# One quarter of the last values load in six transfers, with unread products moved

## The chip, the cores and the metric

The kernel runs on one core of a Trainium2 chip. The metric is device time in microseconds (us), the median of several executions. The profile is of one execution.

## The reference

The input is one decode step: x of 8 rows by 512. It is normalized to xn, and the output is x plus two branches of xn:

```python
q = (xn @ wq).reshape(8, 1, 32, 128).transpose(0, 2, 1, 3)
scores = einsum("bhqd,bhkd->bhqk", q, repeat(k_cache, 4)) * 128 ** -0.5
o = einsum("bhqk,bhkd->bhqd", softmax(scores), repeat(v_cache, 4))
A = o.transpose(0, 2, 1, 3).reshape(8, 1, 4096) @ wo
h = xn @ w1 + b1
B = (h * tanh(softplus(h))) @ w2
return x + A + B
```

The caches have 8 rows, 8 heads, 8192 positions and 128 values each, all float32: 268 MB of keys and 268 MB of values. Each byte is read once and used for the four query heads of its group.

## The kernel before

**Loads.** All large loads are issued by SyncE (SP) from one list. `plan` puts a load into `queue`; `pump` issues the loads at the head of the list for as long as their place is free; `release` gives a place free after the last use and calls `pump`. There are three places in SBUF: "a" (tile `kva`, 16 rows of 1024 floats a partition), "b" (`kvb`, 20 rows) and "w" (`kvw`, 4 rows). One load of keys or values is 8 MB, 128 partitions of 64 KB. Every `dma_start` of a load stands on line 121. The framework puts in all waits, and gives each transfer one of eight completion semaphores in turn (by number 102, 103, 105, 107, 108, 109, 110, 100).

**Work.** The batch of 8 and the 8 KV heads are cut into 16 packs of two batch rows (b = 0, 1) by two heads. For pack p the loop scores the keys of (p, b) (`scores`, L353), does the softmax (`maximum`, `exponents`, `fold`, `weights`) and multiplies the values of (p - 1, b) (`values`, L460, then `gather` L471 and L473). In `values` a round is four products into four column strips; the trace has two records for each float32 product, so a whole batch is 64 records.

**The tail** (L695 on) is the change's place. The values of the last pack's first batch come in place "b", those of its second batch in "a", in two parts by columns: three quarters, and the last quarter (16 KB in each of 128 partitions). Then come w2 in four parts (`W2_PARTS`, 8, 8, 8 and 4 KB a partition) and between them the last wo in two halves (8 KB each):

```python
    plan_v(PACKS - 1, 0, "b")
    plan_v(PACKS - 1, 1, "a", ((0, 3 / 4), (3 / 4, 1)))
    W2_PARTS = ((0, 2), (2, 4), (4, 6), (6, 7))
    for k, (lo, hi) in enumerate(W2_PARTS):
        plan("w2", "b", w2, ((lo / W2R, hi / W2R),))
        if 0 < k < 3:
            plan_wo(PAIRS - 1, (((k - 1) / 2, k / 2),))
```

So SP issues, in order: the values' three quarters, the last quarter, w2 part 0, w2 part 1, wo half 0, w2 part 2, wo half 1, w2 part 3, and the output (L719). TensorE's order in the tail is that of the code: `values(0)`, `sums`, `merge` (L488), `add_up` (L548), `values(1)` in two calls, `down` part 0 (L628), two unread products (`keep_busy`, L639), `merge`, `turn` (L514, copies on L526 and L528), `down` part 1, half of `last_outputs` (L562), `down` part 2, the other half, `down` part 3. All of it but the unread products adds into one PSUM tile H or leads to it; L718 copies H out.

`keep_busy(n)` multiplies `ones` by `acc` into C[0], which nothing reads any more. Each engine's order is held to that of the code by the loop at the end of the kernel.

Of the kernel before, what the change touches and what calls it, by code (L numbers as in the profile page):

```python
# [13 lines left out]
P = 128  # L14
# [26 lines left out]
PACKS = PAIRS * NP  # L41
R = P // G
HE = P // 2
# [29 lines left out]
def kernel(  # L73
# [12 lines left out]
    nc = tc.nc  # L86
# [9 lines left out]
    queue = []  # L96
    taken, landed = {}, {}

    def rows_of(blocks):

        return blocks.rearrange("j p f -> (j p f)").rearrange("(p f) -> p f", p=P)
# [9 lines left out]
        del taken[next(at for at, w in taken.items() if w == what)]  # L111
        pump()

    def plan(what, at, blocks, parts=((0, 1),), lo=0):

        rows = rows_of(blocks)
        n = rows.shape[1]
        t = place[at][:, lo : lo + n]

        def load(cols):  # L120
            nc.sync.dma_start(t[:, cols], rows[:, cols])
            return t

        for first, end in parts:
            cols = slice(round(first * n), round(end * n))
            queue.append((what, at, lambda cols=cols: load(cols)))


    sc = const.tile([P, 512], F32, name="sc")
# [7 lines left out]
    def blocks_of(src, p, b):  # L137
        i, k = divmod(p, NP)
        lo = ((k * PB + b) * HKV + 2 * i) * NB
        return src[lo : lo + KN]  # L140
# [3 lines left out]
    def plan_k(p, b):  # L144
        if (p, b) == (0, 1):
            plan(("k", p, b), "a", blocks_of(kT, p, b))
        else:
            up[0] = KX * BW - up[0]
            plan(("k", p, b), "b", blocks_of(kT, p, b), lo=up[0])

    def plan_v(p, b, at, parts=((0, 1),)):
        plan(("v", p, b), at, blocks_of(v, p, b), parts)

    def plan_wq(i):
        plan(("wq", i), "w", wq[i * CC : (i + 1) * CC])
# [11 lines left out]
    for p in range(PACKS):  # L167
        for b in range(PB):
            plan_k(p, b)
            if (p, b) in between:  # L170
                what, i = between[p, b]
                (plan_wq if what == "wq" else plan_wo)(i)
            if p > 0:
                plan_v(p - 1, b, "a")
    plan_v(PACKS - 1, 0, "b")
    plan_v(PACKS - 1, 1, "a", ((0, 3 / 4), (3 / 4, 1)))
    W2_PARTS = ((0, 2), (2, 4), (4, 6), (6, 7))
    for k, (lo, hi) in enumerate(W2_PARTS):
        plan("w2", "b", w2, ((lo / W2R, hi / W2R),))
# [274 lines left out]
    def values(b, vt, lo=0, hi=ROUNDS):  # L454


        for k in range(lo, hi):
            for c in range(G):
                j = G * k + c
                nc.tensor.matmul(  # L460
                    O[b][Q * c : Q * (c + 1), :],
                    pt[:, b, j % 2, j // 2].rearrange("p t e h -> p (t e h)"),
                    vt[:, W4 * DH * j : W4 * DH * (j + 1)],
                    start=(k == 0),
                    stop=(k == ROUNDS - 1),
                )
# [17 lines left out]
    def merge(p, b):  # L484

        i, k = divmod(p, NP)
        at = 168 + b * 2 * REP
        nc.tensor.matmul(M[:, at : at + 2 * REP], OS.pop((p, b)), hsel, start=True, stop=True)  # L488
        if b == PB - 1:
            if k == 0:  # L490
                oT[i] = work.tile([P, 2, REP, B], F32, name="oT")
            nc.vector.tensor_mul(  # L492
                oT[i][:, :, :, k * PB : (k + 1) * PB].rearrange("p e h b -> p (e h) b"),
                M[:, 168 : 168 + PB * 2 * REP].rearrange("p (b r) -> p r b", b=PB),
                RT.pop(p).rearrange("p b e h -> p (e h) b"),
            )
# [48 lines left out]
    def add_up():  # L545

        for g in range(G):
            nc.tensor.matmul(  # L548
                H[Q * g : Q * g + B, :P],
                rsel[:, :B],  # L550
                acc[:, g * P : (g + 1) * P],
                start=True,
                stop=False,
            )

    def last_outputs(lo, hi, w):

        for r in range(lo, hi):
            for h in range(2):
                for g in range(G):  # L560
                    at = r * BW + h * D + g * P
                    nc.tensor.matmul(  # L562
                        H[Q * g : Q * g + B, :P],
                        oW[PAIRS - 1][:, r, h, :],
                        w[:, at : at + P],
                        start=False,
                        stop=False,
                    )
# [54 lines left out]
    def down(lo, hi, w):  # L623

        for j in range(2 * lo, 2 * hi):
            for g in range(G):
                at = j * D + g * P
                nc.tensor.matmul(  # L628
                    H[Q * g : Q * g + B, :P],
                    aT[:, j, :B],  # L630
                    w[:, at : at + P],
                    start=False,
                    stop=(j == 2 * W2R - 1),
                )

    def keep_busy(n):

        for k in range(n):
            nc.tensor.matmul(C[0][:Q, :], ones[:, :Q], acc, start=True, stop=True)  # L639
# [19 lines left out]
    for p in range(PACKS):  # L659
        for b in range(PB):  # L660
            k = landed.pop(("k", p, b))
# [17 lines left out]
            if (p, b) in between:  # L679
                what, i = between[p, b]  # L680
# [14 lines left out]
    p = PACKS - 1  # L695
# [5 lines left out]
    sums(p, lsel.pop(p))  # L701
    merge(p, 0)
    add_up()
    values(1, landed["v", p, 1], 0, ROUNDS * 3 // 4)
    values(1, landed["v", p, 1], ROUNDS * 3 // 4)
    gather(p, 1)
    w2_sb, wo_sb = landed["w2"], landed["wo", PAIRS - 1]
    down(*W2_PARTS[0], w2_sb)
    keep_busy(2)
    merge(p, 1)  # L710
    turn(PAIRS - 1, tid)
    down(*W2_PARTS[1], w2_sb)
    last_outputs(0, OR // 2, wo_sb)
    down(*W2_PARTS[2], w2_sb)
    last_outputs(OR // 2, OR, wo_sb)
    down(*W2_PARTS[3], w2_sb)
    res = acc[:, :P]
# [59 lines left out]
```

## Time and profile before

| what | value |
|---|---|
| median of 3 runs | 1311.33 us (1311.27 to 1312.54) |
| the profiled execution | 1311.37 us |
| its span | 1309.6 us |
| TensorE matmul busy (PE) | 879.2 us, 67% |
| VectorE busy (DVE) | 385.2 us, 29% |
| ScalarE busy (ACT) | 111.6 us, 9% |
| loads' queue q1 | 561.06 MB, 99.3% of 16 engines |
| mean granted TensorE clock | 0.823 |

The span runs from the program's first instruction to its last; 1.8 us of the execution's time lie around it. Start times below are counted from the span's start. PE is a matmul, PEld its weight load. A line like "L460 PE" names the kernel's line and the engine. "DMA kvb<-in_w" is the transfer of w2 into place "b", "SPq" the issuing by SyncE.

### The profile page before, as it was taken

To read this page: it belongs to the slowest core of one execution; us is meant where nothing else is said; L and a number is where in the kernel's file an instruction comes from. 1 tells how busy PE (TensorE), PEld (TensorE's weight loads), DVE (VectorE), ACT (ScalarE), POOL (GpSimd) and SP (SyncE) were. 2 spreads that over 40 slices of the span, in tenths; PEclk is the share of its full clock that TensorE was granted. 3 is DMA by queue.
4 is the path that set the end of the run, shared out by engine and by line. 5 is a ranking of instruction groups with operands and counts; after the bars stand their busy time and mean duration, and the time that the engine had idled before them with its cause. 6 is when DMAs were issued, how large, how long until landed. Compare 5 with 4: busy or idle time off the path is not lost.

```text
span 1309.6 us, 10699 instructions
## 1 busy us (share of the span) xinstructions
PE 879.2 (67%) x4768; PEld 282.3 (22%) x4768; DVE 385.2 (29%) x590; ACT 111.6 (9%) x294; POOL 4.8 (0%) x10
## 2 busy tenths in 40 slices
PE   4886667866567766677666686665775666766567
PEld 1221112212112221122211222121221221222113
DVE  7150504205050230522305033052320505114051
ACT  1020101001010100101101010010100101001010
POOL 1000000000000000000000000000000000000000
PEclk9887788887789877797777887778887779878778
DMA  9999999999999999999999999999999999999997
GB/s 406 440 427 437 437 427 428 440 433 431 432 435 429 433 437 425 443 421 445 419 442 421 418 448 425 441 421 443 423 437 432 429 433 421 443 427 435 437 425 333
DMA packets 11590, 561.76 MB, mean 429 GB/s; under 512 B 1292, under 2 KB 1424, under 8 KB 1560
## 3 DMA queue, kind: packets, MB, share of 16 engines
q1 hardware_dynamic: 11520, 561.06, 99.3%
q8 instruction: 37, 0.61, 0.2%
q14 instruction: 9, 0.07, 0.0%
q10 hardware_dynamic: 24, 0.02, 0.0%
HBM read 561.01 MB, written 0.07 MB: 428 GB/s over the span
## 4 chain that ended last, share of the span: by engine, by line
DMA 61%; PE 35%; DVE 3%; issue 0%; ACT 0%; SPq 0%; DVEq 0%; ACTq 0%
DMA kvb<-in_kT 52%; PE c L353 30%; PE o L460 3%; DMA kva<-in_v 3%; DMA kva<-in_kT 3%; DMA kvb<-in_w 2%; DMA kvb<-in_v 2%; DVE raw L412 1%; DVE pt L430 1%; PE h L312 0%; PE o L581 0%; PE s L365 0%; DVE raw L421 0%; DVE nm L379 0%; DVE os L473 0%
## 5 line engine op out<-in xcount | busy, mean ns | idle before, releaser
L353 PE MATMUL c<-kvb,qT 128*64 128x512 f32 x1984 | 500.7, 669 | 334.4 <-DMA kvb<-in_kT 302.3
L353 PEld LDWEIGHTS c<-kvb,qT 128*64 128x64 f32 x1984 | 161.7, 154 | 673.3 <-issue 424.4
L460 PE MATMUL o<-kva,pt 128*32 128x512 f32 x1984 | 251.4, 665 | 26.2 <-DMA kva<-in_v 26.2
L379 DVE TENSOR_REDUCE nm<-s 128x1 f32<-128x1024 f32 x16 | 19.6, 1225 | 454.7 <-PE s L365 454.7
L412 DVE STREAM_TRANSPOSE raw<-e 128x2048 f32<-128x2048 f32 x32 | 116.2, 3630 | 14.3 <-ACT e L404 12.7
L460 PEld LDWEIGHTS o<-kva,pt 128*32 128x32 f32 x1984 | 67.1, 121 | 200.3 <-issue 161.1
L360 ACT COPY sc<-c 128x512 f32<-128x512 f32 x32 | 18.7, 585 | 1003.4 <-PE c L353 1003.4
L404 ACT ACTIVATE e<-s,nms 128x512 f32<-128x512 f32 x128 | 86.2, 685 | 126.3 <-DVE nms L393 66.8
L492 DVE TENSOR_TENSOR oT<-m,r 128x16 f32<-128x16 f32 x16 | 2.8, 174 | 234.1 <-PE m L488 234.1
L471 DVE TENSOR_SCALAR os<-o,isel 128x128 f32<-128x128 f32 x32 | 11.2, 351 | 160.1 <-PE o L460 160.1
L430 DVE TENSOR_TENSOR pt<-raw 64x256 f32<-64x256 f32 x128 | 53.6, 419 | 2.0
L365 PE MATMUL s<-sc,csel 64*128 64x512 f32 x128 | 38.0, 672 | 8.4 <-ACT sc L360 8.4
L421 DVE TENSOR_TENSOR raw<-raw 128x1024 f32<-128x1024 f32 x32 | 39.2, 1226 | 1.1
L340 DVE TENSOR_TENSOR qT<-qc,bsel 128x1024 f32<-128x1024 f32 x32 | 37.7, 1219 | 0.0
L473 DVE SCALAR_TENSOR_TENSOR os<-o,isel,os 128x128 f32<-128x128 f32 x96 | 33.7, 351 | 3.4
L404 ACT ACTIVATION_READ_ACCUMULATOR e<-s,nms 128x1 f32 x128 | 26.0, 203 | 0.0
L380 PE MATMUL m<-ident,nm 128*1 128x128 f32 x16 | 4.3, 270 | 21.2 <-DVE nm L379 21.2
L312 PE MATMUL h<-kvw,xnT 128*64 128x512 f32 x64 | 17.6, 699 | 0.0
L488 PEld LDWEIGHTS m<-hsel,os 128*128 128x128 f32 x64 | 9.5, 188 | 28.5 <-issue 24.4
L323 DVE TENSOR_SCALAR e<-h 128x512 f32<-128x512 f32 x16 | 9.9, 684 | 17.2 <-PE h L312 17.2
L488 PE MATMUL m<-hsel,os 128*128 128x8 f32 x64 | 12.4, 266 | 3.1 <-DVE os L473 1.6
L353 PE MATMUL c<-kva,qT 128*64 128x512 f32 x64 | 14.0, 593 | 0.6 <-DMA kva<-in_kT 0.6
(100 smaller groups left out, 164.6 us busy)
## 6 DMA issues: line engine op xcount, KB each, us to landing
kvw<-in_wq SPq DMA_DIRECT2D x4, 2048.0 KB, 30.4
kvw<-in_wo SPq DMA_DIRECT2D x3, 2048.0 KB, 29.6
kva<-in_v SPq DMA_DIRECT2D x1, 6144.0 KB, 26.1
kva<-in_w SPq DMA_DIRECT2D x1, 3584.0 KB, 15.7
kvb<-in_w SPq DMA_DIRECT2D x3, 1024.0 KB, 21.0
kva<-in_v SPq DMA_DIRECT2D x1, 2048.0 KB
kvw<-in_wo SPq DMA_DIRECT2D x2, 1024.0 KB, 24.8
kvb<-in_w SPq DMA_DIRECT2D x1, 512.0 KB
```

The source lines that it names most:

```text
L340: nc.vector.tensor_mul(qT[:, b], qc[:, k * PB + b] .rearrange("p r (o h) -> p r o h", o=1) .to_broadcast([P, KR, KN, REP]), bsel.rearrange ...
L353: nc.tensor.matmul(C[b][HE * c : HE * (c + 1), :], t[:, r], k[:, r * BW + c * 512 : r * BW + (c + 1) * 512], start=(r == order[0]), stop=( ...
L360: nc.scalar.copy(sc, C[b])
L365: nc.tensor.matmul(S[:, c * 512 : (c + 1) * 512], csel[HE * c : HE * (c + 1), b].rearrange("p u b h -> p (u b h)"), sc[HE * c : HE * (c + ...
L379: nc.vector.tensor_reduce(nm, S, axis=AX.X, op=ALU.max, negate=True)
L404: nc.scalar.activation(ex[:, :, s, :], S[:, c * 512 : (c + 1) * 512].rearrange("p (t f) -> p t f", t=HT), AF.Exp, bias=NMS[p][:, s : s + 1 ...
L412: nc.vector.transpose(raw.rearrange("p (m t r) -> p t m r", m=TW, t=HT), ex.rearrange("p t s (q m) -> p t m (s q)", m=TW),)
L421: nc.vector.tensor_add(raw[:, :, :n], raw[:, :, :n], raw[:, :, n:])
L430: nc.vector.tensor_add(pt[rows, b, c].rearrange("p m t e h -> p (m t) e h")[:, :, e], raw[rows, :, at : at + REP], raw[rows, :, V8 + at : ...
L460: nc.tensor.matmul(O[b][Q * c : Q * (c + 1), :], pt[:, b, j % 2, j // 2].rearrange("p t e h -> p (t e h)"), vt[:, W4 * DH * j : W4 * DH * ...
L473: nc.vector.scalar_tensor_tensor(os, O[b][:, DH * i : DH * (i + 1)], isel[:, i : i + 1], os, op0=ALU.mult, op1=ALU.add,)
L488: nc.tensor.matmul(M[:, at : at + 2 * REP], OS.pop((p, b)), hsel, start=True, stop=True)
```

## The change

The last quarter of the last values is no longer one transfer over 128 partitions but six: partitions 0 to 63, the even ones of 64 to 127 (32 rows), and the odd ones in four transfers of eight rows (65, 73, ..., 121; then from 67, 69 and 71, each in steps of eight). They carry the same bytes to the same places. Of the unread products, the two between `down` part 0 and `merge` go; four stand after `add_up`, one ahead of `down` part 2 and one ahead of the second half of `last_outputs`.

```diff
-    def plan(what, at, blocks, parts=((0, 1),), lo=0):
+    WHOLE = (slice(0, P),)
+    SPLIT = (slice(0, HE), slice(HE, P, 2)) + tuple(slice(HE + k, P, 8) for k in range(1, 8, 2))
+
+    def plan(what, at, blocks, parts=((0, 1),), lo=0, split=()):
...
-        def load(cols):
-            nc.sync.dma_start(t[:, cols], rows[:, cols])
+        def load(cols, of):
+            for ps in of:
+                nc.sync.dma_start(t[ps, cols], rows[ps, cols])
             return t
 
-        for first, end in parts:
+        for k, (first, end) in enumerate(parts):
             cols = slice(round(first * n), round(end * n))
-            queue.append((what, at, lambda cols=cols: load(cols)))
+            of = SPLIT if k in split else WHOLE
+            queue.append((what, at, lambda cols=cols, of=of: load(cols, of)))
...
-    plan_v(PACKS - 1, 1, "a", ((0, 3 / 4), (3 / 4, 1)))
+    plan_v(PACKS - 1, 1, "a", ((0, 3 / 4), (3 / 4, 1)), split=(1,))
...
     add_up()
+    keep_busy(4)
     values(1, landed["v", p, 1], 0, ROUNDS * 3 // 4)
     values(1, landed["v", p, 1], ROUNDS * 3 // 4)
     gather(p, 1)
     w2_sb, wo_sb = landed["w2"], landed["wo", PAIRS - 1]
     down(*W2_PARTS[0], w2_sb)
-    keep_busy(2)
     merge(p, 1)
     turn(PAIRS - 1, tid)
     down(*W2_PARTS[1], w2_sb)
     last_outputs(0, OR // 2, wo_sb)
+    keep_busy(1)
     down(*W2_PARTS[2], w2_sb)
+    keep_busy(1)
     last_outputs(OR // 2, OR, wo_sb)
     down(*W2_PARTS[3], w2_sb)
```

More of the change, by code (lines that the diff above doesn't have):

```diff
@@ L149, in plan_k, with plan_v @@
             plan(("k", p, b), "b", blocks_of(kT, p, b), lo=up[0])
-    def plan_v(p, b, at, parts=((0, 1),)):
-        plan(("v", p, b), at, blocks_of(v, p, b), parts)
+    def plan_v(p, b, at, parts=((0, 1),), split=()):
+        plan(("v", p, b), at, blocks_of(v, p, b), parts, split=split)
     def plan_wq(i):
```

## The prediction

> **What bounds the kernel now.** I read the page first, for the chain that ended last:
>
> ```profile
> ## 3 DMA queue, kind: packets, MB, share of 16 engines
> q1 hardware_dynamic: 11520, 561.06, 99.3%
> q8 instruction: 37, 0.61, 0.2%
> ...
> DMA 61%; PE 35%; DVE 3%; issue 0%; ACT 0%; SPq 0%; DVEq 0%; ACTq 0%
> ```
>
> The loads' queue q1 keeps the 16 DMA engines busy for 99.3% of the span. Transfers make 61% of the chain that ended last. The change touches only the last 48 us, so next came the chain of waits from 1255 us on:
>
> ```profile
> 1278.39 0.43 SPq L121
> 1278.82 0.04 issue
> 1278.87 27.12 DMA kvb<-in_w
> 1305.99 0.04 issue
> 1306.03 0.67 PE h L628 x16
> 1306.70 0.02 issue
> 1306.72 0.29 DVE acc L718
> ```
>
> The last part of w2 lands at 1305.99; sixteen small products, one copy and the output transfer follow, and nothing else. What TensorE does before that is seen in the timeline (start, duration, and in brackets the idle time before):
>
> ```profile
> 1287.54 9.67 PE L460 MATMUL o<-kva,pt 128*32 128x512 f32 x64 [3.64 <-DMA kva<-in_v]
> 1297.91 1.88 PE L639 MATMUL c<-acc,ones 128*32 128x512 f32 x4
> 1299.72 0.39 PE L488 MATMUL m<-hsel,os 128*128 128x8 f32 x2
> 1304.80 1.06 PE L562 MATMUL h<-kvw,oW 128*8 128x128 f32 x32 [0.35 <-DMA kvw<-in_wo]
> 1306.03 0.62 PE L628 MATMUL h<-kvb,aT 128*8 128x128 f32 x16 [0.17 <-DMA kvb<-in_w]
> ```
>
> TensorE waits for both last weight parts, but only by 0.35 and 0.17 us: it is nearly as late as the transfers.
>
> **Why the last transfer lands when it does.** A transfer over 128 partitions adds 1 to its semaphore for each of 16 DMA engines. The trace has those times; for the last part of w2 they are 1301.9, 1301.9, 1302.0, 1302.1, 1302.3, 1302.9, 1303.1, 1303.7, then 1303.9, 1304.0, 1304.1, 1304.1, 1305.6, 1305.7, 1305.8, 1306.0. The engines carry equal bytes and end 4.1 us apart. The packet records tell why: a packet begins 3 to 4 ns before its engine's previous one ends, so the records sort into 16 chains. The 37 packets of q8 (16 KB of TensorE's instructions each, about 1.0 us, and the data packet behind takes 2.9 instead of 2.42 us) fall on eight chains in rotation. Those eight are the last eight above; the eight free of q8 are the first eight. The mean of the 16 is 1303.7, so no sharing out of these bytes could gain over 2.3 us.
>
> **Step 1, the split.** The last quarter is 128 rows of 16 KB: eight packets an engine, 0.611 us each (its first engine counts at 1288.2, 4.9 us after the same engine counted for the three quarters). Now 64 rows give each engine four, 32 rows two, and four transfers of eight rows give eight engines one each: the trace shows that eight rows (x) add only eight counts, and four rows (b1) only four. Eight engines carry ten rows, eight carry six: 2 x 0.611 = 1.22 us more and less. Which eight? b1's four packets lie on four chains without q8, which by chance would be 70 in 1820, 4%. If the eight-row parts use those four and the other four free ones, the early eight move from 1303.7 at the latest to 1304.9 and the late eight from 1306.0 to 1304.8. Last landing 1304.9: **a gain of 1.1 us**. Five more counting packets of 9 ns on the early engines are nothing.
>
> The Trainium skill ("DMA: Bandwidth & Descriptors", section "Why a DMA increments its semaphore by 16 and not by 1") says that a transfer on fewer engines from this queue takes the lowest-numbered ones; by that the eight would include b1's four, and the gain would be the same.
>
> **Step 2, the issues.** Six issues instead of one, at 1263.09. At 0.33 to 0.43 us each (the issues of this tail but one, 1.21) they end by 1265.7; SP's next is held until 1272.8 by the landing of v's first batch. Hidden by that wait; its cost is zero up to 7 us. The eight completion semaphores are used in turn, though, and a new use waits for the old:
>
> ```profile
> SPq L719 <- DMA kva<-in_v: 8.2, 1, 8.2
> ```
>
> The output's issue has nothing to do with kva; it waits because its semaphore was that of the three quarters. Five more transfers shift the turn by five. The second part of w2 (now issued 1276.29) gets that semaphore and goes out at 1287.5; the first half of wo waits for the 64 rows (about 1287.5 + 4 x 0.61 = 1289.9), the third w2 part for the 32 rows (1291.2), the rest for eight-row parts of about then. From issue to first packet is 0.9 us (output: 1307.04 to 1307.93), so the second w2 part is there at 1288.9. The first engine to end the part before counts at 1290.6 + 1.22 = 1291.8 if early, 1292.8 - 1.22 = 1291.6 if late. Cover 2.7 us: no engine runs dry. Without it each us would be paid.
>
> **Step 3, TensorE.** Four unread products after add_up take eight halves of 0.43 us (L639: four in 1.88) at full clock: 1283.9 to 1287.3, in the 3.64 us of waiting. The clock shows what for:
>
> ```profile
> 1283.90:1287.50 3.60, 0.00 (x1) 0.00 (x0) 0.00 (x0) 0.00 (x0) 0.00 (x0) 0.79 0.88 378
> 1287.50:1293.00 5.50, 5.46 (x28) 1.38 (x32) 0.00 (x0) 0.00 (x0) 0.00 (x0) 0.52 0.97 408
> 1293.00:1297.00 4.00, 4.00 (x40) 1.06 (x36) 0.00 (x0) 0.00 (x0) 0.00 (x0) 1.00 1.02 420
> ```
>
> (Third number from the end: granted clock.) At 0.52 a round of four takes 0.85 us, at 1.00 0.43. Warm throughout, values(1) ends at 1287.5 + 16 x 0.43 = 1294.4 instead of 1297.0; the last quarter, in by about 1291.3, is needed at 1292.7. The two products that held L488 from 1298.8 (end of gather) to 1299.7 are gone. The extra waits for six semaphores instead of one are in front of that slack. So turn and last_outputs come some 3.5 us earlier, into waits for w2 and wo. The two new single products (0.86 us each) stand there: first half of last_outputs done about 1300.1, product to 1301.0, third w2 part about 1301.2 to 1302.3, product to 1303.1, second half of wo due at 1304.75 - 1.1 = 1303.6. Cover 0.5 us. If TensorE fell to half clock there, what follows 1300.1 (0.86 + 1.06 + 0.86 + 1.06 + 0.62 = 4.5 us) would take 8.9 and end at 1309.0, against 1306.65 now: 2.4 us lost. Now the clock is 1.00 there with TensorE busy for 3.13 of the last 4.00 us (table of stretches), and the products fill gaps, so I take zero.
>
> **Sum.** The profiled execution took 1311.37 us, its span 1309.6; the median of the three runs is 1311.33, so one may be taken for the other. Steps 2 and 3 give zero, step 1 gives 1.1: **1310.2 us**, 0.08% less. About 0.2% (2.6 us) is what measuring this kernel can tell from no change, so this is "same".
>
> **Rivals.** *Shared destinations.* Now sixteen engines write to 128 partitions at once. After the split they write to 64, then eight engines to eight rows among the upper 64. If two engines then share a way in that one filled, an eight-row packet takes 1.22 instead of 0.61 us: 4 x 0.61 = 2.4 us on the early engines, 1304.9 + 2.4 = 1307.3, or +1.4: 1312.7. If the 64 rows are halved too, another 2.4: 1315.1, slower by 0.3%; the 2 to 4 us between early and late engines keep most of them apart there. It decides from 1.1 us on, a packet of 0.89 us. Against it: x's eight packets of 2 KB went to eight neighbouring partitions at once and took 81 to 118 ns, where b1's 1792 B took 74, that is 85 for 2 KB. For it: 2 KB is short, and no row shows a long burst. 27%.
>
> The Trainium skill speaks against the change here: "SBUF — State Buffer", section "Door 1", has 64 partitions reach eight of sixteen ports, at 196 GB/s measured where 128 got 328. By that the lower rows and the eight-row parts would run at about half rate, and the sum would be the 1315.1 above or less; this trace has no such transfer.
>
> *The wrong eight.* If eight rows fall on the engines that are late, 1306.0 + 1.22 = 1307.2: 1312.5. 8%; b1's chains speak against it.
>
> *Parts held apart.* If the program orders the interleaved partition sets one behind another, SP stands behind each landing: 32 rows go out at 1289.9, then four times some 2.4 us (issue 0.43, start 0.9, packet 0.61, count 0.5), and w2 at about 1301 instead of 1275; the 13 us of w2 and wo then end near 1315, +9: 1320. The column parts of w2 are issued without such waits (1274.92 to 1278.87); for partitions nothing shows. 5%.
>
> *Half clock in the tail*, as above: 1313.7. 4%. *Nothing moves* (rows shared otherwise): 1311.3. 6%.
>
> **Chances.** The forecast has 50%. Its own range is 1309.0 (all of the 2.3) to 1311.3. With the rivals, 1309.0 to 1313.9 reaches to the middle of the sharing and leaves out its upper half and the ordering, some 18%. Faster by over 0.2% would need more than all the imbalance: 7%, for what I do not see. Slower by over 0.2%: upper part of the sharing (10), ordering (5), the wrong eight and sharing together (3): 18%. Between: 75%.
>
> **What would show it.** Right: the 16 counts of the last w2 part within about 3 us, last near 1304.9, after six counts for the quarter by 1291.5; L460 of values(1) near 6.9 us; SP's second w2 issue at 1287.5. Wrong: eight-row packets over 0.9 us (sharing), late engines later than 1306 (wrong eight), w2 issued after 1290 (ordering), L562 or L628 at double length (clock).

## The result and the profile after

| kernel | median | runs |
|---|---|---|
| before | 1312.02 us (1311.27 to 1313.62) | 6 |
| after | 1323.13 us (1321.84 to 1325.57) | 6 |

The ratio is 1.0088, with a 95% interval of 1.0077 to 1.0098: the change makes the kernel slower by about 11 us. The forecast was 1310.2 us in a range up to 1313.9. The prediction was wrong. The profiled execution of after took 1321.87 us, 10.5 us more than that of before, and its span (1320.1 us) is also 10.5 us longer.

The page of after, its queues and the engines of the chain that ended last, still names the same bound:

```profile
q1 hardware_dynamic: 11568, 561.06, 99.4%
q8 instruction: 37, 0.61, 0.2%
...
DMA 58%; PE 37%; DVE 4%; issue 0%; ACT 0%; SPq 0%; ACTq 0%; DVEq 0%
```

The bytes are equal, and the queue is still counted as busy for all of the span. The 48 new packets are the counting packets of five more transfers (six transfers count 64 times where one counted 16 times). So "busy" says nothing here of speed. The chain of waits of after (start, duration, what) shows the same ending, later:

```profile
1263.64 37.42 DMA kva<-in_v
...
1302.82 13.78 DMA kvb<-in_w
1316.64 0.67 PE h L634 x16
...
1317.34 0.29 DVE acc L726
```

The last part of w2 lands at 1316.60 instead of 1305.99, 10.6 us later, and what follows it takes as long as before. So the whole loss has to be found ahead of 1316.6, among the transfers. The chain has one new member, a values transfer (`kva`) that ends at 1301.06. The timeline of after (start, duration, instruction; in brackets the idle time before it and what ended it) shows who waits for the values:

```profile
1285.27 5.29 PE L645 MATMUL c<-acc,ones 128*32 128x512 f32 x8
1290.53 5.36 PE L466 MATMUL o<-kva,pt 128*32 128x512 f32 x48
1290.55 0.33 SPq L126 DMA_DIRECT2D kvb<-in_w  x1
...
1303.37 3.28 PE L466 MATMUL o<-kva,pt 128*32 128x512 f32 x16 [7.49 <-DMA kva<-in_v]
...
1315.41 1.06 PE L568 MATMUL h<-kvw,oW 128*8 128x128 f32 x32 [0.55 <-DMA kvw<-in_wo]
1316.64 0.62 PE L634 MATMUL h<-kvb,aT 128*8 128x128 f32 x16 [0.17 <-DMA kvb<-in_w]
```

The values' three quarters are in at 1290.5 (before: 1287.5), and the last quarter at 1303.2, against 1292.4 before: 10.9 us later. From there to the end the distance is about the same as before (13.4 us to the landing of the last w2 part, 13.6 before). The table of stretches of after says how fast the transfers went (stretch, length, busy time of PE, PEld, DVE, ACT and POOL, granted clock, DMA share, GB/s):

```profile
1285.00:1290.00 5.00, 5.00 (x18) 1.28 (x17) 0.00 (x0) 0.00 (x0) 0.00 (x0) 0.66 0.92 216
1290.00:1295.00 5.00, 5.00 (x46) 1.46 (x48) 0.00 (x0) 0.00 (x0) 0.00 (x0) 1.00 1.16 174
1295.00:1300.00 5.00, 0.88 (x12) 0.00 (x0) 0.00 (x0) 0.00 (x0) 0.00 (x0) 0.93 0.86 113
1300.00:1304.00 4.00, 0.63 (x4) 0.23 (x8) 0.00 (x0) 0.00 (x0) 0.00 (x0) 0.50 0.92 262
1304.00:1310.00 6.00, 4.98 (x62) 2.69 (x57) 1.58 (x5) 0.00 (x0) 0.00 (x0) 0.82 1.01 422
```

The DMA share stays near 1 while the rate falls to 113 GB/s: the engines hold packets all the time, and each packet takes longer. The same table of before:

```profile
1285.00:1290.00 5.00, 2.46 (x12) 0.59 (x16) 0.00 (x0) 0.00 (x0) 0.00 (x0) 0.60 0.98 415
1290.00:1295.00 5.00, 5.00 (x40) 1.38 (x36) 0.00 (x0) 0.00 (x0) 0.00 (x0) 0.72 1.01 421
1295.00:1300.00 5.00, 5.00 (x62) 1.89 (x54) 1.40 (x4) 0.00 (x0) 0.00 (x0) 1.00 1.01 418
```

After moves (5 x 216 + 5 x 174 + 5 x 113 + 4 x 262) / 19 = 188 GB/s over the 19 us from 1285 to 1304. At some 420 GB/s that data would take 8.5 us, so 10.5 us are lost there, which is the whole difference.

The packet records say which packets are long. Of the 128 packets of 16 KB in the split, 108 take 1.1 to 2.5 us instead of 0.61. But the 48 KB packets of the three quarters, which the change does not touch, take up to 3.2 us instead of 1.82 on the engines that are late, and w2's 8 KB packets beside the split take 0.5 to 1.3 us instead of 0.31.

### The profile page after: what moved, and what is told of

The parts are those of the page before. It is cut to its first block, busy times and chain, and to the rows that moved or that the text cites. A ratio compares the mean times of both kernels' runs of the same rounds, so it can differ in the third digit from the quotient of the medians.

```text
span 1320.1 us, 10726 instructions
## 1 busy us (share of the span) xinstructions
PE 881.2 (67%) x4776; PEld 283.3 (21%) x4776; DVE 385.0 (29%) x590; ACT 111.7 (8%) x294; POOL 4.8 (0%) x10
## 4 chain that ended last, share of the span: by engine, by line
DMA 58%; PE 37%; DVE 4%; issue 0%; ACT 0%; SPq 0%; ACTq 0%; DVEq 0%
DMA kvb<-in_kT 51%; PE c L359 31%; PE o L466 3%; DMA kva<-in_v 3%; DMA kva<-in_kT 2%; DVE raw L418 1%; DMA kvb<-in_w 1%; DVE pt L436 1%; DVE nm L385 1%; PE s L371 1%; PE o L587 0%; PE h L318 0%; DVE raw L427 0%; DVE os L479 0%; ACT sc L366 0%
## 5 line engine op out<-in xcount | busy, mean ns | idle before, releaser
L466 PE MATMUL o<-kva,pt 128*32 128x512 f32 x1984 | 245.7, 652 | 27.1 <-DMA kva<-in_v 27.1
L466 PE MATMUL o<-kvb,pt 128*32 128x512 f32 x64 | 10.0, 792 | 8.0 <-DMA kvb<-in_v 8.0
```

The source lines that it names most:

```text
L466: nc.tensor.matmul(O[b][Q * c : Q * (c + 1), :], pt[:, b, j % 2, j // 2].rearrange("p t e h -> p (t e h)"), vt[:, W4 * DH * j : W4 * DH * ...
```

## The experiments

The question was first which part of the change does this, then what it is in that part, then what sets its size. In the expectations, S stands for where the split's rows lie, K for the moved products, T for the number of transfers and the shifted turn of the semaphores. Later, two accounts of the size stand against each other: R has everything in flight slowed while any engine works on a split transfer, O has only the split transfer's own packets slowed. Each kernel computes all of the output. The kernel before took 1311.4 to 1311.5 us in the same groups of runs; each diff is against the kernel after.

### Which part of the change

**whole**: one transfer for the last quarter, the products as in after.

```diff
-    plan_v(PACKS - 1, 1, "a", ((0, 3 / 4), (3 / 4, 1)), split=(1,))
+    plan_v(PACKS - 1, 1, "a", ((0, 3 / 4), (3 / 4, 1)))
```

> The last quarter in one transfer over 128 partitions again, the unread products as changed. Theory S (the split's transfers write to few partitions at a time, and several DMA engines share what one of them fills, so packets of 16 KB take 1.1 to 2.5 us instead of 0.61): nothing of that is left, so the time of before, 1312.0 within 0.2%, the last w2 part landing near 1306. Theory K (the moved products cost it): near 1323. Theory T (the turn of the semaphores holds the issues of w2 and wo back): the turn is that of before, 1312.

Measured: 1311.54 us, ratio to before 0.9999 (0.9989 to 1.0009). Without the split the loss is gone, and the moved products are worth nothing that can be measured either way.

**oldbusy**: the six transfers, the unread products where before had them.

```diff
-    keep_busy(4)
     values(1, landed["v", p, 1], 0, ROUNDS * 3 // 4)
...
+    keep_busy(2)
     merge(p, 1)
...
-    keep_busy(1)
     down(*W2_PARTS[2], w2_sb)
-    keep_busy(1)
```

> The six transfers, with the unread products where they were before. S: the whole loss, 1322 to 1324, with values(1) ending after 1303. K: 1312. T: 1322 to 1324.

Measured: 1321.9 us, 1.008 (1.0065 to 1.0095). The split alone brings the loss of after.

**columns**: six transfers in the same proportions (2048, 1024 and four times 256 columns), each over all 128 partitions.

```diff
-            of = SPLIT if k in split else WHOLE
-            queue.append((what, at, lambda cols=cols, of=of: load(cols, of)))
+            cuts = (0, 2048, 3072, 3328, 3584, 3840, 4096) if k in split else (0, cols.stop - cols.start)
...
+                for a, b in zip(cuts, cuts[1:]):
+                    load(slice(cols.start + a, cols.start + b), WHOLE)
```

> Six transfers of the same sizes as in the change (half, quarter and four sixteenths of the last quarter), but cut by columns: each over all 128 partitions. The count, the issues and the turn of the semaphores are those of the change. S: 1312 within 0.3%, packets of 8, 4 and 1 KB at 26 GB/s an engine or a little less. T: 1323, since SP still waits for landings before each part of w2 and wo. K: 1323.

Measured: 1311.78 us, 1.0005 (0.9995 to 1.0014). It has the same number of issues and the same shift of the turn, and loses nothing that can be measured. So it is not the count of transfers but their partitions.

### What it is in the split

**three** leaves out the eight-row transfers; **by4** keeps four of them, with other rows in each; **lower** mirrors the split, so that the upper half goes first and the odd rows of 0 to 63 go by eights.

```diff
three:
+    SPLIT = (slice(0, HE), slice(HE, P, 2), slice(HE + 1, P, 2))
by4 (the first two sets as in after):
+    ... + tuple(slice(k, k + 29, 4) for k in (65, 67, 97, 99))
lower:
+    SPLIT = (slice(HE, P), slice(0, HE, 2)) + tuple(slice(k, HE, 8) for k in range(1, 8, 2))
```

> The eight-row transfers replaced by one of the 32 odd rows: 64, 32 and 32 rows, each over 16 engines. S: no engine has more rows than another, but all sixteen write to 64 partitions at a time, so a 16 KB packet takes about 1.2 us instead of 0.61 and eight of them 9.6 instead of 4.9: up to 4.7 us over before, less what the 4 us between early and late engines keep apart: 1314 to 1317. If the eight-row transfers are the whole loss: 1312. If it is the number of rows on the early engines: 1312.

> Six transfers of the same 64, 32 and four times 8 rows as in the change; only which odd rows go together differs: 65, 69, ..., 93, then from 67, 97 and 99, in steps of four instead of eight. S, if what is shared is a group of four neighbouring partitions (64 to 67, 68 to 71 and so on) or what it hangs on: the eight rows of a transfer now lie in eight groups, not in eight of which two pairs hang together, so the eight-row packets fall from 1.2 to 2.5 us to between 0.61 and 1.2, and the time to 1314 to 1320. If eight-row transfers are slow whatever their rows: 1323. T: 1323.

> The change mirrored: first partitions 64 to 127, then the even rows of 0 to 63, then the odd ones of 0 to 63 in four transfers of eight rows (1, 9, ..., 57 and so on). The engines with ten rows write their eight-row parts to the lower half. S, with engines of a 128-row transfer each writing their own rows in order (first eight engines the lower half): the eight-row parts no longer meet the w2 packets of the engines with six rows, which keep 0.31 us for 8 KB instead of up to 1.29: 1316 to 1321. If that does not matter: 1322 to 1324, as in the change.

Measured: three 1321.45 us, 1.0074 (1.0059 to 1.0089); by4 1322.48 us, 1.0083 (1.0068 to 1.0098); lower 1322.37 us, 1.0075 (1.0058 to 1.0092). All three are above the outcome named first for each (up to 1317, 1320 and 1321 us); by4 and lower came out near the others named (1323; 1322 to 1324). In by4 the eight-row packets take mostly 1.1 to 1.6 us where after has up to 2.5, and the time does not move; in three they are absent, and it moves hardly. So the eight-row transfers, in which my rival had seen the main danger, are not where most of the time goes. In lower the late engines' 48 KB packets take up to 4.8 us: either half coming first slows them.

**halves**: two transfers, of partitions 0 to 63 and 64 to 127. **parity**: two transfers of 64 rows as well, but of the even and the odd partitions of all 128.

```diff
halves:
+    SPLIT = (slice(0, HE), slice(HE, P))
parity:
+    SPLIT = (slice(0, P, 2), slice(1, P, 2))
```

> The last quarter in two transfers, partitions 0 to 63 and 64 to 127. S: the same as with 64, 32 and 32 rows, 1314 to 1317, since each half is one side of the 128 partitions. If transfers of few rows are slow by themselves: between 1312 and that.

> The last quarter in two transfers of 64 rows, the even and the odd partitions of all 128. S, if it matters where the rows lie and not how many there are: the 64 rows of each transfer reach all that 128 do, so packets stay near 0.61 us and the time is 1312 within 0.3%. If 64 rows are slow whichever they are: as with the two halves, 1314 to 1317.

Measured: halves 1320.39 us, 1.0064 (1.0049 to 1.0079); parity 1311.53 us, 1.0002 (0.9993 to 1.0011). This pair carries the verdict: same bytes, same number of transfers, as many rows for each engine, and 9 us between them. The table of stretches of halves:

```profile
1284.00:1288.00 4.00, 4.00 (x18) 1.29 (x18) 0.00 (x0) 0.00 (x0) 0.00 (x0) 1.00 0.76 164
1288.00:1292.00 4.00, 0.79 (x5) 0.20 (x8) 0.00 (x0) 0.00 (x0) 0.00 (x0) 0.88 1.00 221
1292.00:1296.00 4.00, 4.00 (x32) 1.07 (x28) 0.00 (x0) 0.00 (x0) 0.00 (x0) 0.70 0.94 215
1296.00:1300.00 4.00, 2.21 (x24) 0.37 (x15) 0.00 (x0) 0.00 (x0) 0.00 (x0) 1.00 1.01 195
```

and that of parity:

```profile
1284.00:1288.00 4.00, 3.47 (x14) 1.17 (x15) 0.47 (x2) 0.00 (x0) 0.00 (x0) 0.66 0.85 365
1288.00:1292.00 4.00, 4.00 (x31) 1.16 (x33) 0.00 (x0) 0.00 (x0) 0.00 (x0) 0.92 1.00 420
1292.00:1296.00 4.00, 4.00 (x44) 1.24 (x40) 0.00 (x0) 0.00 (x0) 0.00 (x0) 1.00 1.02 422
1296.00:1300.00 4.00, 2.95 (x44) 1.67 (x40) 1.58 (x5) 0.00 (x0) 0.00 (x0) 1.00 1.01 420
```

The last column is the one to read. Halves has a mean of 199 GB/s over 16 us, parity 407: 16 x (1 - 199 / 407) = 8.2 of the 9 us lie in these four rows. The packet records, as medians of the packets that begin in 2 us:

| from | parity: 48, 16, 8 KB | halves: 48, 16, 8 KB |
|---|---|---|
| 1282 | 1.82, 0.611, - | 3.05, 0.96, - |
| 1286 | -, 0.611, 0.309 | 3.55, 1.24, - |
| 1290 | -, 0.611, 0.309 | -, 1.19, 0.63 |
| 1296 | -, -, 0.312 | -, 1.54, 0.64 |
| 1300 | -, -, 0.312 | -, -, 0.312 |

From the moment the first engine begins a packet of a half until the last engine has ended its own, all packets take about twice as long, those of the 128-row transfers before and behind as well.

### What sets the size

If that is the rule, the loss does not depend on the split's bytes alone. The rule was made from halves, so only smaller splits test it. The engines enter the split one after another (over some 4.2 us, as far as they stand apart in the tail of before) and leave it so. At full rate, from the first entry to the last exit, that is 4.2 us and the time of the split data; at half rate it lasts twice as long, and the loss is that same time again: for a quarter 4.2 + 4.9 = 9.1 us, for an eighth 4.2 + 2.4 = 6.6, for a sixteenth 4.2 + 1.2 = 5.4. If only the split's own packets are slowed, it is 4.9, 2.4 and 1.2 us. **eighth** and **sixteenth** have only the last eighth or sixteenth in halves:

```diff
+    SPLIT = (slice(0, HE), slice(HE, P))
eighth:
+    plan_v(PACKS - 1, 1, "a", ((0, 3 / 4), (3 / 4, 7 / 8), (7 / 8, 1)), split=(2,))
sixteenth:
+    plan_v(PACKS - 1, 1, "a", ((0, 3 / 4), (3 / 4, 15 / 16), (15 / 16, 1)), split=(2,))
```

> Only the last eighth of the last values (1 MB) in two halves by partitions; the eighth before it in one transfer. Theory R: from the first engine's entry into a half to the last engine's exit, everything in flight moves at half the rate, also other transfers' packets. In before the engines run 4.2 us apart, and 1 MB takes 2.45 us, so the stretch is 6.6 us of full-rate work and takes twice that: 1311.4 + 6.6 = 1318.0. (By the same rule the quarter in halves: 4.2 + 4.9 = 9.1, measured 9.0.) Rival O: only the split's own packets take twice as long: 1311.4 + 2.45 = 1313.9.

> Only the last sixteenth (512 KB) in two halves. R: 4.2 + 1.2 = 5.4, 1316.8. O: 1311.4 + 1.2 = 1312.6.

Measured against before:

| split in halves | everything in flight | own packets only | measured (by the ratio's interval) |
|---|---|---|---|
| quarter | +9.1 | +4.9 | +9.0 (+6.4 to +10.4) |
| eighth | +6.6 | +2.4 | +6.8 (+3.9 to +7.9) |
| sixteenth | +5.4 | +1.2 | +4.3 (+2.2 to +5.1) |

"Own packets only" lies below every interval. "Everything in flight" holds for the quarter, from which it was made, and for the eighth; for the sixteenth it is about 1 us too high, just outside. The counts on the semaphores show the slow stretch itself. From the first engine's count for the transfer ahead of the two halves to the last engine's count for the second half, it is 18.1 us in halves (1283.5 to 1301.6), 13.9 in eighth (1285.4 to 1299.4) and 9.8 in sixteenth (1288.1 to 1297.8). Half of that is 9.0, 7.0 and 4.9 us; these three profiled executions took 9.1, 6.8 and 5.2 us more than the median of before. A quarter of the bytes still costs half of the loss, and the table of stretches of eighth shows that the slow time outlasts the data:

```profile
1288.00:1292.00 4.00, 3.44 (x32) 1.07 (x36) 0.00 (x0) 0.00 (x0) 0.00 (x0) 1.00 1.05 227
1292.00:1296.00 4.00, 2.77 (x28) 0.58 (x20) 0.00 (x0) 0.00 (x0) 0.00 (x0) 1.00 1.01 219
```

Its first engine has counted for both halves at 1290.1, its last at 1299.4.

**twoqueues** was to bring both halves in hand at the same time: the upper half goes out from ScalarE's queue.

```diff
+    SPLIT = (slice(0, HE), slice(HE, P))
-                nc.sync.dma_start(t[ps, cols], rows[ps, cols])
+                queue_of = nc.scalar if ps.start == HE else nc.sync
+                queue_of.dma_start(t[ps, cols], rows[ps, cols])
```

> The quarter in two halves, the lower one issued by SyncE and the upper one by ScalarE, so that an engine has both in its hands at once and can take packets from them in turn. If the slowness comes from all engines writing to one side at a time, it falls: 1311.5 to 1316. If a transfer to 64 partitions is slow by itself, or the queues are served one after the other: 1320 to 1321, as with the halves from one queue.

Measured: 1325.87 us, 1.0105 (1.0088 to 1.0122), above both outcomes named. The timeline of twoqueues:

```profile
1262.73 0.54 SPq L127 DMA_DIRECT2D kva<-in_v  x1
1262.73 0.55 ACTq L127 DMA_DIRECT2D kva<-in_v  x1
1282.88 2.03 SPq L127 DMA_DIRECT2D kvb<-in_w  x2
```

Both halves are issued at 1262.73, but only SP's half stood behind what SP had queued. ScalarE's packets began at 1267.05 and took turns with SP's 64 KB and 48 KB packets until 1282. The values' first batch then landed at 1280.8 instead of 1272.8, and w2, which waits for its place, was issued at 1282.9 instead of 1275. The two halves were never in hand together, so the run says nothing about pairing them. It does show each half alone among 128-row transfers, the upper one in the first two rows of its table of stretches, the lower one in the last two:

```profile
1272.00:1276.00 4.00, 0.00 (x0) 0.00 (x0) 1.61 (x6) 0.00 (x0) 0.00 (x0) 0.50 0.83 193
1276.00:1280.00 4.00, 0.00 (x0) 0.00 (x0) 0.00 (x0) 0.00 (x0) 0.00 (x0) 0.50 0.93 233
1296.00:1300.00 4.00, 0.07 (x1) 0.00 (x0) 0.00 (x0) 0.00 (x0) 0.00 (x0) 0.87 0.86 172
1300.00:1304.00 4.00, 3.66 (x20) 0.99 (x24) 0.00 (x0) 0.00 (x0) 0.00 (x0) 0.50 0.99 207
```

One half is enough to slow the rest.

**spread** was the attempt at a better version: the change's sizes, 64, 32 and four times eight rows, each spread over all 128 partitions.

```diff
+    SPLIT = (slice(0, P, 2), slice(1, P, 4)) + tuple(slice(k, P, 16) for k in (3, 7, 11, 15))
```

> The same shares of rows as in the change (64 over 16 engines, 32 over 16, four times 8 over eight engines), but each transfer spread over all 128 partitions: the even rows; 1, 5, ..., 125; then 3, 19, ..., 115 and from 7, 11 and 15 in steps of 16. R: no transfer stays on one half, so nearly all of the 11 us goes; the eight-row transfers still write eight rows in groups of few, so 1311 to 1314. If the moved rows also help, as I forecast of the change: 1310.3. If few rows or few engines cost by themselves: 1314 to 1323.

Measured: 1315.97 us, 1.003 (1.0021 to 1.004): 7 us better than after, still 4.5 us behind before, and above the 1311 to 1314 that the rule for halves gave. The 64 and 32 rows now go at 0.611 us a packet. The eight-row packets take 1.1 us in the median, w2's packets beside them 0.59, and the table of stretches of spread shows the same half rate for 8 us:

```profile
1288.00:1292.00 4.00, 4.00 (x40) 1.30 (x44) 0.00 (x0) 0.00 (x0) 0.00 (x0) 1.00 1.02 240
1292.00:1296.00 4.00, 1.36 (x16) 0.15 (x8) 0.00 (x0) 0.00 (x0) 0.00 (x0) 1.00 1.00 217
```

(8 x (1 - 229 / 420) = 3.6 us of the 4.5.) So a half is not the only set of rows that slows the rest. Whether it is the place of the eight rows or that they are so few, on eight engines, no run tells apart. The 1.1 us that rows moved from late to early engines might bring never showed, and no version here beats the kernel before.

## Why the prediction was wrong

**Step 1, the split, is the step that failed**, and in it the term of a packet's duration: 0.611 us for every 16 KB packet, wherever its row lies. The runs showed 1.1 to 2.5 us for most, and rates of 113 to 216 GB/s from 1285 to 1300. The last w2 part's 16 counts run from 1311.4 to 1316.6, 5.2 us apart, where "about 3 us, last near 1304.9" was to show it right. The number of engines was seen correctly: the six transfers' counts are 16, 16 and four times eight. Which eight engines get the eight-row parts was not: two of the first three engines to end the 32 rows begin w2's 8 KB packets at once (1288.56 and 1288.85), so they carried six rows and not ten. This was worth little beside the packets' durations.

**The rival "Shared destinations" forecast the slow packets, and its price was the second error.** Its sign, eight-row packets over 0.9 us, came true. It counted only the split's own packets (+1.4 to +3.8 us) and took the 2 to 4 us between early and late engines as what would "keep most of them apart". The runs show the reverse: the distance lengthens the slow stretch. For halves alone the two terms of the rule stood in the prediction, 4.1 us as the distance of the 16 counts and 4.9 us as the time of the quarter: 9.0 us, or 1320, outside the range. The evidence against the rival, x's eight packets of 81 to 118 ns, was read from one short transfer, and does not hold even for it: in the trace of after five of the same eight packets take 825 to 1622 ns. It did not say what 16 KB packets do beside other transfers.

The Trainium skill ("SBUF — State Buffer", section "Door 1") was cited as speaking against the change, and it was right about the rate: it has 64 partitions of one half at 196 GB/s (a transfer of 1 MiB), halves measured a mean of 199. The same section gives a table of which partitions share a port. By it parity's sets reach all 16 ports, and the eight-row sets of after and of spread four; parity at full rate and the slow eight-row packets agree with that. No run shows a port itself, though, and which engine writes to which partitions was not settled either. In all runs a partition also fixes where its row is read in HBM (row p starts p times 64 KB into the load), so the runs do not tell slow writing from slow reading. What exactly is shared stays argued. Measured is only that a 64-row half slows everything in flight, and that 64 alternate rows do not.

**Step 2, the issues, held in kind.** SP issued the six transfers from 1263.03 to 1266.8 without waiting for one of them, so "Parts held apart" did not happen. The second w2 part got the turn of the three quarters, as worked out, at 1290.55 instead of 1287.5, because these landed 3 us late. (So the sign given for the ordering, w2 issued after 1290, came up for another reason.) The late issues cost nothing: from 1275 us until the last w2 part the packet records of after leave none of the 16 engines without a packet. Columns shares the five more issues and the shift of the turn, and takes 1.0005 of before.

**Step 3, TensorE, held where it mattered.** Values(1) ran warm (48 records in 5.36 us) and then stood for 7.49 us for the last quarter. The four products took 5.29 us, not 3.4, as the clock granted was 0.66 in their stretch; the later landing covered it. "Half clock in the tail" did not come: L568 and L634 took 1.06 and 0.62 us as before. In whole, without the split, values(1) takes 7.08 us (about 6.9 was forecast), and the time is 0.9999 of before: TensorE's gain is worth nothing while the transfers end last.

**Left open** are the sixteenth, whose median is 1 us below the rule though its profiled execution is within 0.3 us of it, whether the rows' reading or writing is what slows, and why after and its two variants by4 and three cost 1 to 3 us more than halves. Their intervals overlap with that of halves.

## What to carry to other kernels

A transfer cut by partitions must be looked at for where its rows lie, not for how many bytes each engine gets: a contiguous half of the partitions ran at half rate here, 64 alternate rows of all 128 at full rate, and eight rows 16 partitions apart were slow again. Price such a cut by all that is in flight beside it, from the first engine's entry to the last one's exit, so that engines that stand far apart make it dearer. Where the DMA share is 1, look at GB/s and at the duration of a known packet before calling the engines well used.

## What the runs showed of the hardware

- A transfer to partitions 0 to 63 or 64 to 127 slows 128-row transfers beside it too: 48 KB packets from 1.82 to 3.5 us, 8 KB packets from 0.31 to 0.64 us (halves).
- A transfer issued from ScalarE's queue did not stand behind the transfers that SP had queued before it: its packets began 4.3 us after the issue, among theirs, and the values' first batch landed 8 us later (twoqueues).
- A transfer of eight rows that are 16 partitions apart also ran slowly, at 1.1 us a 16 KB packet in the median instead of 0.61, and w2's 8 KB packets beside it at 0.59 us (spread).
